# Q and K transposed by DMA instead of TensorE and VectorE in a fused attention and feed-forward kernel

## Chip, cores, metric

One core of one Trainium2 chip. The metric is the device time of one execution in microseconds (us), the median of several runs. Brackets behind a time give the lowest and the highest run, those behind a ratio a 95% interval.

## The reference, cut to what matters

Block-sparse attention (4 batches, 8 heads, 768 tokens, head size 64), then a gated feed-forward layer with RMS norm over 512 channels.

```python
scores = scale * q @ k.T                    # per batch and head, masked by blocks of 32 tokens
attn   = softmax(scores);  x = attn @ v     # x: [3072 tokens, 512]
xn     = x / rms(x) * rms_g
out    = (silu(xn @ w_gate) * (xn @ w_val)) @ w_out      # d_ff = 1536
```

## The kernel before

The work goes by *units*: half of the queries of one batch, all eight heads, as four *pairs* of heads. There are 8 units of 12 *steps*. A step issues two score tiles, their exp (ScalarE) and their mask (VectorE); attention times V follows. The feed-forward work of an earlier unit is cut into small items and dealt out between steps to fill TensorE. All of it is one fixed program order per engine.

TensorE needs Q and K with the head dimension on the partitions. The loads bring tokens on the partitions, so every pair is transposed: 24 TensorE transposes into PSUM, then one copy by VectorE.

```python
def load_qk(b, lo, hi):                              # issued on POOL; float32 -> bfloat16
    nc.gpsimd.dma_start(out=qraw[b][:, lo:hi, :], in_=qv[b, :, lo:hi, :])
    nc.gpsimd.dma_start(out=kraw[b][:, lo:hi, :], in_=kv[b, :, lo:hi, :])

def transposes(b, pr, early=False):
    ...
    t_ = ps_s.tile([P, 2, 1024], BF16, name="tqk", tag="s")   # one of the two PSUM slots of the scores
    tt = [t_[:, 0, :], t_[:, 1, :]]
    for i, src in enumerate((qraw[b], kraw[b])):
        for c in range(NC):                          # NC = 6 chunks of 64 columns
            for h in range(2):
                nc.tensor.transpose(out=tt[i][64*h:64*h+64, c*P:(c+1)*P],
                                    in_=src[:, 2*pr+h, c*D:(c+1)*D], identity=ident)
    nc.vector.tensor_copy(out=x, in_=t_[:, :, 0:S])
```

POOL has two roles. It issues all loads, and it makes two small things that TensorE needs at the end of a unit: the squares of the attention output for the RMS norm, and the norm's power of -1/2.

```python
# in av(), once per pair:
    nc.scalar.copy(out=osb[u][:, pr, :], in_=o_)
    nc.gpsimd.tensor_tensor(out=o2s[u][:, pr, :], in0=osb[u][:, pr, :],
                            in1=osb[u][:, pr, :], op=ALU.mult)            # the square
# norm_a(u): TensorE sums the four squares;  norm_b(u), on POOL:
    nc.gpsimd.tensor_tensor(out=rs, in0=ms, in1=nhalf, op=ALU.pow)        # the power, "rs"
```

The plan: `at(step, cost, fn, ...)` puts a piece of work at a step. The cost is the planner's guess of TensorE time. It sets how many feed-forward items are dealt out there.

```python
for b in range(1, B):
    for pr, sl in enumerate((7, 8, 9, 10) if b == 1 else (2, 4, 6, 7)):
        at(3 * (8 * (b - 1) + sl) + 2, 0.95, transposes, b, pr)
    at(3 * 8 * (b - 1) + 1, 0, load_qk, b, 0, H)
    at(3 * (8 * (b - 1) + (1 if b == 1 else 4)) + 1, 0, load_v, b)
at(4, 0, load_wo)
...
    for cost, fn, a in todo:
        fn(*a)
        credit -= cost
        if fn in (transposes, norm_d, norm_e):
            tail = 1.2                               # deal out this much feed-forward work behind it
```

The softmax here doesn't subtract the row's maximum and nothing guards it: scores larger than these inputs give would overflow.

## Time and profile before

| | before |
|---|---|
| median of 3 runs | 387.07 us (386.75 to 387.38) |
| span of the profiled run | 387.4 us |
| TensorE / VectorE / ScalarE / POOL busy | 90% / 67% / 57% / 15% |
| TensorE time of one transpose block | 0.80 us, 12 blocks for batches 1 to 3 |
| VectorE copy of one block | 0.95 us |

From the page of before: busy times, the slices (40 equal parts of the span, busy share in tenths), and the packets of the software queue (POOL's loads) and the hardware queue (SP's transfers).

```profile
span 387.4 us, 6807 instructions
PE 348.7 (90%) x2742; PEld 165.6 (43%) x2742; DVE 259.0 (67%) x539; ACT 222.5 (57%) x353; POOL 59.5 (15%) x88
...
PE   3678788998699899999999999999999999999995
...
DMA  5999960065001500075002400000000000000012
...
q0 software_dynamic: 16208, 14.16, 23.7%
q1 hardware_dynamic: 4020, 6.30, 4.3%
```

TensorE is at 90% or more from slice 15 (136 us) up to the last slice. DMA is full in slices 2 to 5 and partly in 6: weights, V and the first two batches.

From the page's groups (line, engine, operation, out<-in, count, busy us, mean ns, idle before): the transposes and their copy. The count of 13 is the 12 blocks and the first pair of batch 0.

```profile
L168 DVE COPY qkT<-tqk 128x1536 bf16<-128x1536 bf16 x13 | 12.3, 951 | 0.9 <-PE tqk L161 0.9
L161 PE MATMUL tqk<-ident,qb 128*64 128x128 bf16 x156 | 7.2, 229 | 5.5 <-DMA qb<-in_q_dram 4.8
```

From the timeline of before, one block in the steady state (start, length, engine, line):

```profile
192.81 0.53 PE L161 MATMUL tqk<-ident,qb 128*64 128x128 bf16 x12
...
193.61 0.82 PE L405 MATMUL yp<-wo,hp 128*128 128x512 bf16 x3
...
194.33 0.95 DVE L168 COPY qkT<-tqk 128x1536 bf16<-128x1536 bf16 x1
```

The block starts at 192.81 and the next TensorE work at 193.61: 0.80 us.

From the list of waits of TensorE between 60 us and the end (us, times, longest): score matmuls that waited for a copy, since the transposes held a score slot.

```profile
PE s__1097 L235 <- DVE qkT L168: 1.0, 1, 1.0
...
PE s__941 L235 <- DVE qkT L168: 0.8, 1, 0.8
...
PE s__1252 L235 <- DVE qkT L168: 0.7, 1, 0.7
...
PE s__2797 L235 <- DVE qkT L168: 0.4, 1, 0.4
PE s__1952 L235 <- DVE qkT L168: 0.4, 1, 0.4
```

These sum to 3.3 us.

### The profile page before, as it was taken

Reading aid. Unit: us, or ns where it says so; the run is one execution under the profiler, and the core shown is the slowest. Engines: PE = TensorE matmul, PEld = TensorE weight load, DVE = VectorE, ACT = ScalarE, POOL = GpSimd, SP = SyncE. Lnnn points to the kernel's source line nnn. Section 1 sums busy time; section 2 is a strip of 40 time slices with the busy share of each in tenths; the row PEclk is TensorE's granted clock in tenths of the full one; section 3 lists DMA queues with packets and bytes.
Section 4 is the critical chain, followed back from the end, with each engine's and each line's share of the span. In section 5 each row is a group of like instructions: output and inputs, shape, how many; then the busy total and the mean of one; then the engine's idle time right before and its main releaser. Section 6 shows DMA issues by size and latency. Waiting matters only on the chain.

```text
span 387.4 us, 6807 instructions
## 1 busy us (share of the span) xinstructions
PE 348.7 (90%) x2742; PEld 165.6 (43%) x2742; DVE 259.0 (67%) x539; ACT 222.5 (57%) x353; POOL 59.5 (15%) x88
## 2 busy tenths in 40 slices
PE   3678788998699899999999999999999999999995
PEld 1223233444344444454444544444444444455552
DVE  4866675778675877677766777767666776566540
ACT  2357765666556466567666665667667767232331
POOL 8921010131011100021101100010010110100000
PEclk9998867999999999999999999999999999999999
DMA  5999960065001500075002400000000000000012
GB/s 72 178 209 207 205 111 1 0 83 83 0 2 34 77 29 27 2 120 99 3 27 40 71 27 29 2 28 30 0 29 27 29 0 29 28 29 28 29 50 86
DMA packets 20259, 20.88 MB, mean 54 GB/s; under 512 B 1284, under 2 KB 17156, under 8 KB 20228
## 3 DMA queue, kind: packets, MB, share of 16 engines
q0 software_dynamic: 16208, 14.16, 23.7%
q1 hardware_dynamic: 4020, 6.30, 4.3%
q8 instruction: 21, 0.34, 0.4%
q14 instruction: 10, 0.08, 0.1%
HBM read 28.31 MB, written 6.29 MB: 89 GB/s over the span
## 4 chain that ended last, share of the span: by engine, by line
PE 66%; DVE 18%; ACT 11%; issue 3%; DMA 1%; POOL 0%; DVEq 0%; ACTq 0%; POOLq 0%
PE yp L405 13%; PE gp L374 11%; PE vp L391 11%; ACT pt L242 8%; DVE pt L248 6%; PE zw L283 5%; PE oa L267 3%; DVE uu L380 3%; ACT th L378 3%; DVE hp L394 2%; DVE xn L359 2%; PE tqk L161 1%; DVE qkT L168 1%; DMA kb<-in_k_dram 1%; PE vw L391 1%
## 5 line engine op out<-in xcount | busy, mean ns | idle before, releaser
L248 DVE TENSOR_TENSOR pt<-pt,Mk 128x768 bf16<-128x768 bf16 x192 | 101.1, 554 | 23.9 <-ACT pt L242 19.3
L380 DVE SCALAR_TENSOR_TENSOR uu<-th,gp 128x384 bf16<-128x384 bf16 x90 | 49.7, 553 | 57.4 <-ACT th L378 57.1
L378 ACT ACTIVATE th<-gp 128x384 bf16<-128x384 f32 x90 | 44.2, 492 | 62.0 <-PE gp L374 59.9
L405 PE MATMUL yp<-wo,hp 128*128 128x512 bf16 x288 | 76.2, 380 | 0.0
L391 PE MATMUL vp<-xn,wv 128*128 128x384 bf16 x360 | 74.2, 329 | 2.1 <-DVE hp L394 1.8
L374 PE MATMUL gp<-xn,wg 128*128 128x384 bf16 x360 | 74.5, 330 | 1.4 <-DVE xn L359 0.8
L394 DVE TENSOR_TENSOR hp<-uu,vp 128x384 bf16<-128x384 bf16 x90 | 49.8, 553 | 19.6 <-PE vp L391 14.2
L374 PEld LDWEIGHTS <-wg 128*128 128x128 bf16 x384 | 35.4, 99 | 36.5 <-issue 11.0
L391 PEld LDWEIGHTS <-wv 128*128 128x128 bf16 x384 | 35.0, 98 | 31.9 <-issue 12.3
L235 PEld LDWEIGHTS <-qkT 64*128 64x128 bf16 x384 | 14.6, 95 | 55.8 <-issue 47.5
L405 PEld LDWEIGHTS <-hp 128*128 128x128 bf16 x288 | 25.5, 98 | 28.2 <-issue 7.3
L267 PEld LDWEIGHTS <-vb 128*64 128x64 bf16 x384 | 22.6, 116 | 18.6 <-issue 12.1
L411 ACT ACTIVATE yo<-yp 128x512 f32<-128x512 f32 x24 | 14.3, 598 | 20.1 <-PE yp L405 19.8
L283 PE MATMUL zw<-pt,Ez 128*32 128x384 bf16 x384 | 23.3, 352 | 0.0
L359 DVE SCALAR_TENSOR_TENSOR xn<-osb,gcol,fb 128x384 bf16<-128x384 f32 x28 | 15.9, 608 | 0.0
L318 POOL TENSOR_TENSOR rs<-ms,nhalf 128x3 f32<-128x3 f32 x8 | 7.1, 889 | 48.0 <-DVE ms L315 48.0
L267 PE MATMUL oa<-pt,vb 128*64 128x384 bf16 x96 | 13.7, 441 | 0.0
L283 PEld LDWEIGHTS <-Ez 128*32 128x32 bf16 x384 | 7.6, 99 | 13.5 <-issue 11.9
L168 DVE COPY qkT<-tqk 128x1536 bf16<-128x1536 bf16 x13 | 12.3, 951 | 0.9 <-PE tqk L161 0.9
L161 PE MATMUL tqk<-ident,qb 128*64 128x128 bf16 x156 | 7.2, 229 | 5.5 <-DMA qb<-in_q_dram 4.8
L161 PEld LDWEIGHTS <-qb 128*64 128x64 bf16 x192 | 6.6, 116 | 9.7 <-issue 4.8
L183 PE MATMUL mp<-Qvis,Kind 24*128 24x384 bf16 x12 | 5.3, 482 | 3.6 <-DVE Qvis L179 2.5
(556 smaller groups left out, 433.0 us busy)
## 6 DMA issues: line engine op xcount, KB each, us to landing
out_dram<-yo SPq DMA_DIRECT2D x24, 256.0 KB, 2.0
vb<-in_v_dram POOLq DMA_DIRECT2D x4, 768.0 KB, 7.9
qb<-in_q_dram POOLq DMA_DIRECT2D x3, 768.0 KB, 8.0
kb<-in_k_dram POOLq DMA_DIRECT2D x3, 768.0 KB, 10.7
wg<-in_moe_w_gate_dram POOLq DMA_DIRECT2D x2, 768.0 KB, 13.0
wv<-in_moe_w_val_dram POOLq DMA_DIRECT2D x2, 768.0 KB, 16.6
wo<-in_moe_w_out_dram POOLq DMA_DIRECT2D x1, 1536.0 KB, 28.5
qb<-in_q_dram POOLq DMA_DIRECT2D x2, 192.0 KB, 3.5
```

The source lines that it names most:

```text
L161: nc.tensor.transpose(out=tt[i][64 * h:64 * h + 64, c * P:(c + 1) * P], in_=src[:, 2 * pr + h, c * D:(c + 1) * D], identity=ident)
L242: nc.scalar.activation(out=ptiles[n][:, jt, :, :], in_=s_[:, :, 0:TG], func=AF.Exp, scale=SCALE)
L248: nc.vector.tensor_tensor(out=pv, in0=pv, in1=Mk[:, jt, ic * TG:(ic + 1) * TG].unsqueeze(1).to_broadcast([P, 2, TG]), op=ALU.mult)
L267: nc.tensor.matmul(out=o_[64 * e:64 * e + 64, :], lhsT=vb[:, 2 * pr + e, jt * D:(jt + 1) * D], rhs=pt_[:, jt, e, :], start=(jt == 0), stop ...
L283: nc.tensor.matmul(out=zwt[u][32 * c:32 * c + 32, :], lhsT=Ez[:, pr, :], rhs=pt_[:, 2 * j2 + par, e, :], start=(pr == 0 and j2 == 0), stop ...
L359: nc.vector.scalar_tensor_tensor(out=xns[u][:, pr, :], in0=osb[u][:, pr, :], scalar=gcol[:, pr:pr + 1], in1=fb[i], op0=ALU.mult, op1=ALU.mult)
L374: nc.tensor.matmul(out=gp, lhsT=wg[:, c, f * P:(f + 1) * P], rhs=xns[u][:, c, :], start=(c == 0), stop=(c == NP - 1))
L378: nc.scalar.activation(out=th, in_=gp, func=AF.Tanh, scale=0.5)
L380: nc.vector.scalar_tensor_tensor(out=uu, in0=th, scalar=1.0, in1=gp, op0=ALU.add, op1=ALU.mult)
L391: nc.tensor.matmul(out=vp, lhsT=wv[:, c, f * P:(f + 1) * P], rhs=xns[u][:, c, :], start=(c == 0), stop=(c == NP - 1))
L394: nc.vector.tensor_tensor(out=hps[u][:, f, :], in0=uu, in1=vp, op=ALU.mult)
L405: nc.tensor.matmul(out=yp, lhsT=hps[u][:, f, t * P:(t + 1) * P], rhs=wo[:, f, :], start=(f == 0), stop=(f == NF - 1))
```

## The change

The intent: take 12 transpose blocks off the busiest engine and 12 copies off VectorE, using a DMA transpose on the SP queue, which is nearly idle. A DMA transpose wants a pair's two heads interleaved by chunk, so the loads write them so: four DMAs per pair (Q and K, two heads each) with rows of 128 B in SBUF, where before two DMAs per batch wrote rows of 768 B.

```diff
-    qkpool = ctx.enter_context(tc.tile_pool(name="qkpool", bufs=6))
+    qkpool = ctx.enter_context(tc.tile_pool(name="qkpool", bufs=8))
...
+    def load_pair(b, pr):
...
+        for t, src in ((qraw[b], qv), (kraw[b], kv)):
+            dst = t[:, 2 * pr:2 * pr + 2, :].rearrange("p h w -> p (h w)").rearrange(
+                "p (c h d) -> p h c d", c=NC, h=2)
+            sp = src[b, :, 2 * pr:2 * pr + 2, :].rearrange("p h (c d) -> p h c d", c=NC)
+            for h in range(2):
+                nc.gpsimd.dma_start(out=dst[:, h], in_=sp[:, h])
...
+    def transposes_dma(b, pr):
+        x = qkpool.tile([P, 2, S], BF16, name="qkT", tag="qkT")
+        qk[(b, pr)] = x
+        for i, src in enumerate((qraw[b], kraw[b])):
+            nc.sync.dma_start_transpose(
+                out=x[:, i, :].rearrange("q (c p) -> q c p", c=NC),
+                in_=src[:, 2 * pr:2 * pr + 2, :].rearrange("p h w -> p (h w)"))
...
     for b in range(1, B):
-        for pr, sl in enumerate((7, 8, 9, 10) if b == 1 else (2, 4, 6, 7)):
-            at(3 * (8 * (b - 1) + sl) + 2, 0.95, transposes, b, pr)
-        at(3 * 8 * (b - 1) + 1, 0, load_qk, b, 0, H)
+        for pr in range(NP):
+            at(3 * (8 * (b - 1) + pr) + 1, 0, load_pair, b, pr)
+            at(3 * (8 * (b - 1) + pr + (3 if b == 1 else 2)) + 1, 0, transposes_dma, b, pr)
```

## The prediction

> **What bounds the kernel now.** TensorE. The page gives it 348.7 of 387.4 us (90%); VectorE 67%, ScalarE 57%, POOL 15%. In the table by stretches TensorE is busy 19.2 to 19.8 us of every 20 from 160 us on, but only 16.8 to 18.6 between 80 and 160 us. The chain of waits is 66% TensorE. DMA is full (about 205 GB/s written) from 8 to 54 us and mostly idle later.
>
> **What goes away.** Twelve blocks of 24 TensorE transposes. The timeline around single blocks shows 0.80 us from a block's first matmul to the next work: 12 x 0.80 = 9.6 us of TensorE. Twelve VectorE copies of 951 ns = 11.4 us. The list of waits from 60 us on has five waits of TensorE for such a copy (score matmuls that needed the PSUM slot which the transposes held), 3.3 us in all, and transposes that waited 0.7 us for the exp. All this is on the in-order TensorE stream: 13 to 14 us. VectorE's 11.4 us is mostly off the chain.
>
> **What is added.**
> (a) Loads: a pair's Q and K become 4 DMAs of 768 packets of 128 B written (256 B read) in place of packets of 768 B: 12,288 per batch for 2,048. Software-queue packets cost 23.7% x 16 x 387 / 16,208 = 90 ns each on average. If a small one costs 45 to 90 ns (estimate), a pair takes 9 to 17 us of all 16 engines, a batch 35 to 70 us, where its period is about 87 us. POOL issues cost 0.72 to 0.98 us whatever the size: 48 for 6, +36 us of a 15% busy engine.
> (b) 24 DMA transposes of 128x768. The Trainium skill, "VectorE: DVE Perf Modes", section "The three transpose paths", gives 1309 ns for 128x128 by DMA; no run here shows it yet. Six blocks are then at most 8 us, 24 transposes up to 190 us of the SP queue, which now issues only 24 stores. They are issued 14 or more steps (about 3.5 us each) before their first use.
>
> **Critical path.** Steady state hides both. The tight place is batch 1: its loads share the full DMA queue with weights, V and the output weight. I estimate that its last pair lands at 85 to 110 us; its first use is at step 33, about 112 us in before, less the gain. So perhaps 0 to 5 us of new waiting there, or more at the bad end. Stores behind transposes on SP can be late by a few us; three output buffers cover that.
>
> **Prediction.** 13.5 us off, some 2 us given back by new waits on ScalarE and VectorE and by batch 1: 376 us. Range 368 to 386. Faster by over 2%: 65%; within 2%: 22%; slower: 13%.
>
> **What would show it right.** TensorE busy about 339 us, the 951 ns copies down from 13 to 1, no score matmul waiting for them; gain spread over 73 to 248 us; VectorE near 247 us; packets near 47,000; DMA transposes under 8 us each; no score matmul waiting on a transpose DMA. Up to 60 us the two traces should be alike.
>
> **What would make it wrong.** Small packets or transposes that take several times my estimates, so that score matmuls of batch 1 wait for a transposed tile; POOL blocked when too many descriptors are outstanding, so that the squares or the norm's power come late and TensorE waits at the norm; SP held so long that stores, then ScalarE's output copies, stall; or TensorE's removed time turning into waits for exp and mask, so that the gain shrinks below 2%.

## More of the kernel before

Last, POOL's timeline of before where the start's loads and the squares of unit 0 (`o_322`) meet:

```profile
17.50 0.92 POOL L70 DMA_DIRECT2D qb<-in_q_dram  x1
...
25.32 0.83 POOL L273 TENSOR_TENSOR o_322<-osb 128x384 bf16<-128x384 f32 x1 [6.03 <-ACT osb L272]
26.10 0.94 POOL L75 DMA_DIRECT2D vb<-in_v_dram  x1
27.03 1.02 POOL L133 DMA_DIRECT2D wo<-in_moe_w_out_dram  x1
...
37.34 0.82 POOL L273 TENSOR_TENSOR o_322<-osb 128x384 bf16<-128x384 f32 x1 [5.39 <-ACT osb L272]
43.96 0.83 POOL L273 TENSOR_TENSOR o_322<-osb 128x384 bf16<-128x384 f32 x1 [5.80 <-ACT osb L272]
49.97 1.06 POOL L318 TENSOR_TENSOR rs<-ms,nhalf 128x3 f32<-128x3 f32 x1 [5.18 <-DVE ms L315]
```

POOL never waits for a DMA here. Each square waits only for ScalarE's copy, and the power of unit 0 comes at 49.97 us.

## The result and the profile after

392.38 us median (392.12 to 393.07, 3 runs) against 387.07. The ratio to before is 1.0141, interval 1.0117 to 1.0165. A ratio is the mean time of one kernel's runs over that of the other's of the same rounds, so not quite the ratio of the medians quoted. The change made the kernel 1.4% slower: clear of the noise, though less than the 2% at which a run counts as slower here.

The page after:

```profile
span 390.7 us, 6305 instructions
PE 332.0 (85%) x2426; PEld 157.2 (40%) x2454; DVE 249.2 (64%) x527; ACT 222.1 (57%) x353; POOL 93.4 (24%) x130
...
PE   2687508798879999998989898999899899999995
...
DMA  5999999008866930053999520000000000000012
...
q0 software_dynamic: 47600, 14.16, 35.0%
q1 hardware_dynamic: 23220, 11.02, 12.2%
```

The removed work is gone: VectorE 259 to 249 us, TensorE 348.7 to 332.0. (This trace lacks 28 records of the output matmuls. The page's idle time before these is 3.5 us, so TensorE's time is nearer 335.5; plain16 below, with the same matmul list and all records, has 335.9.) But slices 5 and 6 of TensorE's row, 39 to 59 us, have fallen to 5 and 0, from 7 and 8 before: a hole. The list of waits of TensorE names it:

```profile
PE zw L312 <- POOL o_324 L293: 13.9, 1, 13.9
PE vp L411 <- DVE hp L414: 5.4, 11, 0.9
...
PE gp L394 <- DVE uu L400: 4.3, 9, 1.2
```

TensorE waits 13.9 us once, for a POOL square. POOL's timeline after, the same place as above:

```profile
25.41 0.82 POOL L293 TENSOR_TENSOR o_324<-osb 128x384 bf16<-128x384 f32 x1 [4.48 <-ACT osb L292]
26.19 0.88 POOL L83 DMA_DIRECT2D qb<-in_q_dram  x1
28.98 0.82 POOL L83 DMA_DIRECT2D qb<-in_q_dram  x1 [1.92 <-DMA wv<-in_moe_w_val_dram]
32.24 0.82 POOL L83 DMA_DIRECT2D kb<-in_k_dram  x1 [2.44 <-DMA wg<-in_moe_w_gate_dram]
35.96 0.82 POOL L83 DMA_DIRECT2D kb<-in_k_dram  x1 [2.90 <-DMA wv<-in_moe_w_val_dram]
...
37.72 1.03 POOL L145 DMA_DIRECT2D wo<-in_moe_w_out_dram  x1
38.74 0.90 POOL L293 TENSOR_TENSOR o_324<-osb 128x384 bf16<-128x384 f32 x1
...
42.94 0.84 POOL L293 TENSOR_TENSOR o_324<-osb 128x384 bf16<-128x384 f32 x1
...
47.33 0.82 POOL L83 DMA_DIRECT2D kb<-in_k_dram  x1 [1.92 <-DMA vb<-in_v_dram]
57.01 0.82 POOL L83 DMA_DIRECT2D kb<-in_k_dram  x1 [8.86 <-DMA wo<-in_moe_w_out_dram]
57.84 0.84 POOL L293 TENSOR_TENSOR o_324<-osb 128x384 bf16<-128x384 f32 x1
63.26 1.05 POOL L338 TENSOR_TENSOR rs<-ms,nhalf 128x3 f32<-128x3 f32 x1 [4.57 <-DVE ms L335]
```

The bracket is POOL's idle time and what ended it. At the issue of a small load POOL waits until an *earlier, unrelated* DMA has landed: the weights, V, and last for 8.86 us the output weight `wo`. The last square of unit 0 stands behind that in POOL's order and runs at 57.84 us; the power follows at 63.26 us, 13.3 us later than before.

Counting POOL's load issues in program order shows the rule: each waits for the completion of the DMA issued eight before it. The instruction list agrees: POOL's DMA issues take eight completion semaphores (DMASW0 to DMASW7) in turn, and from the ninth on each waits on its own. The semaphore numbers in the traces of before and after show the same. So the 17th to 19th DMA (pair 1) wait for the 9th to 11th (three weight pieces), the 28th for the 20th (V), the 29th (last of pair 3) for the 21st (`wo`). The Trainium skill, "DMA: Bandwidth & Descriptors", section "Why a DMA increments its semaphore by 16 and not by 1", asks for "One semaphore per in-flight slot, not one per stream"; here the program has eight such slots.

The second reading is a table of unit lengths: the distance from one `rs` on POOL's timeline to the next (us). "First" is the first `rs`, "tail" the rest of the span.

| kernel | first | 0-1 | 1-2 | 2-3 | 3-4 | 4-5 | 5-6 | 6-7 | sum of units | tail |
|---|---|---|---|---|---|---|---|---|---|---|
| before | 50.0 | 36.84 | 44.52 | 43.37 | 41.89 | 43.89 | 40.70 | 36.13 | 287.3 | 50.1 |
| after | 63.3 | 31.93 | 42.28 | 41.40 | 42.36 | 42.34 | 42.35 | 35.84 | 278.5 | 48.9 |

The late start costs 13.3 us. The units give back 8.8 and the tail 1.2, so the span is 3.3 us longer (390.7 against 387.4). The medians differ by more, 5.3 us: the profiled execution of before took 389.08 us, more than any of its three timed runs. (The plan deals the feed-forward work out over units, so early columns are best read in sum.) Column 5-6 is strange: that unit had no transposes in either kernel, and no loads or DMA transposes run in it, yet it takes 42.35 in place of 40.70 us. Something costs 1.65 us a unit that is neither DMA nor transposes.

Unit 0-1 needs a caution: the TensorE clock that was granted there differs between runs (0.88 of full speed in before, 0.98 in after; from unit 2-3 to 6-7 it was 1.00 in both). before and loads_only (below) have the same matmul list, and their unit 0-1 takes 36.84 us at 0.88 and 34.31 us at 0.99. So some 2.5 us of a difference between two sums can be clock.

### The profile page after: what moved, and what is told of

It reads as the page before. It is cut to its first block, busy times and chain, and to the rows that moved or that the text cites. A ratio compares the mean times of both kernels' runs of the same rounds, so it can differ in the third digit from the quotient of the medians.

```text
span 390.7 us, 6305 instructions
## 1 busy us (share of the span) xinstructions
PE 332.0 (85%) x2426; PEld 157.2 (40%) x2454; DVE 249.2 (64%) x527; ACT 222.1 (57%) x353; POOL 93.4 (24%) x130
## 2 busy tenths in 40 slices
DMA packets 70850, 25.58 MB, mean 65 GB/s; under 512 B 58020, under 2 KB 67748, under 8 KB 70820
## 3 DMA queue, kind: packets, MB, share of 16 engines
q0 software_dynamic: 47600, 14.16, 35.0%
q1 hardware_dynamic: 23220, 11.02, 12.2%
## 4 chain that ended last, share of the span: by engine, by line
PE 50%; DVE 19%; ACT 11%; DMA 10%; issue 4%; POOL 4%; POOLq 0%; DVEq 0%; ACTq 0%
PE gp L394 10%; PE yp L425 10%; PE vp L411 9%; ACT pt L262 7%; DVE pt L268 7%; DMA wo<-in_moe_w_out_dram 5%; DMA wv<-in_moe_w_val_dram 5%; DVE uu L400 5%; PE zw L303 4%; ACT th L398 3%; DVE xn L379 3%; DVE hp L414 3%; PE oa L287 1%; PE vw L411 1%; PE gw L394 1%
## 5 line engine op out<-in xcount | busy, mean ns | idle before, releaser
L425 PE MATMUL yp<-wo,hp 128*128 128x512 bf16 x260 | 70.8, 381 | 3.5 <-issue 3.1
L411 PEld LDWEIGHTS <-wv 128*128 128x128 bf16 x384 | 36.0, 99 | 35.3 <-issue 14.5
L287 PEld LDWEIGHTS <-vb 128*64 128x64 bf16 x384 | 21.4, 114 | 18.0 <-issue 11.0
L83 POOL DMA_DIRECT2D kb<-in_k_dram x24 | 19.6, 819 | 16.3 <-DMA wo<-in_moe_w_out_dram 8.9
L431 ACT ACTIVATE yo<-yp 128x512 f32<-128x512 f32 x24 | 14.3, 597 | 15.3 <-PE yp L425 13.6
L83 POOL DMA_DIRECT2D qb<-in_q_dram x24 | 20.5, 856 | 1.9 <-DMA wv<-in_moe_w_val_dram 1.9
L312 PE MATMUL zw<-o_324,Ew 128*32 128x384 bf16 x4 | 0.8, 372 | 13.9 <-POOL o_324 L293 13.9
L316 DVE COPY zs<-zw 128x384 f32<-128x384 f32 x8 | 4.4, 551 | 12.7 <-PE zw L312 12.7
L287 PE MATMUL oa<-pt,vb 128*64 128x384 bf16 x96 | 12.2, 404 | 0.0
```

The source lines that it names most:

```text
L83: nc.gpsimd.dma_start(out=dst[:, h], in_=sp[:, h])
L287: nc.tensor.matmul(out=o_[64 * e:64 * e + 64, :], lhsT=vb[:, 2 * pr + e, jt * D:(jt + 1) * D], rhs=pt_[:, jt, e, :], start=(jt == 0), stop ...
L411: nc.tensor.matmul(out=vp, lhsT=wv[:, c, f * P:(f + 1) * P], rhs=xns[u][:, c, :], start=(c == 0), stop=(c == NP - 1))
L425: nc.tensor.matmul(out=yp, lhsT=hps[u][:, f, t * P:(t + 1) * P], rhs=wo[:, f, :], start=(f == 0), stop=(f == NF - 1))
```

## The experiments

I held two theories. **A**: the 13 us at the start come from POOL's order, a load that waits for the DMA eight before it, with a square behind it. **B**: the missing gain in the units comes from the new order of the feed-forward items, because the planner lost the blocks' costs. Rivals: the DMA transposes or the small packets themselves slow the engines or the queue.

### late3: one pair's load moved

```diff
-            at(3 * (8 * (b - 1) + pr) + 1, 0, load_pair, b, pr)
+            at(15 if (b, pr) == (1, 3) else 3 * (8 * (b - 1) + pr) + 1, 0, load_pair, b, pr)
-            at(3 * (8 * (b - 1) + pr + (3 if b == 1 else 2)) + 1, 0, transposes_dma, b, pr)
+            at(24 if (b, pr) == (1, 3) else
+               3 * (8 * (b - 1) + pr + (3 if b == 1 else 2)) + 1, 0, transposes_dma, b, pr)
```

> Edit: the changed kernel with only the load of batch 1's fourth pair moved from step 10 to step 15, and its transposes from step 19 to 24 (first use at step 33). Every packet and every transpose stays. Theory A (POOL waited at a load's issue for the DMA issued eight before it, the output weight, and the square that TensorE needed stood behind it): TensorE's wait for that square falls from 13.9 us to under 2 us, the time to 379 to 384 us. Rival (the full DMA queue itself, or transposes beside loads, delays the start, whatever the order on POOL): the first 64 us stay as long and the time stays above 389 us.

Measured: 378.02 us (377.65 to 381.46), ratio to before 0.9788 (0.9732 to 0.9843). POOL's timeline of late3:

```profile
43.56 0.82 POOL L293 TENSOR_TENSOR o<-osb 128x384 bf16<-128x384 f32 x1 [0.48 <-ACT osb L292]
49.56 1.06 POOL L338 TENSOR_TENSOR rs<-ms,nhalf 128x3 f32<-128x3 f32 x1 [5.18 <-DVE ms L335]
...
51.38 1.75 POOL L83 DMA_DIRECT2D qb<-in_q_dram  x2
...
56.46 0.82 POOL L83 DMA_DIRECT2D kb<-in_k_dram  x1 [2.52 <-DMA wo<-in_moe_w_out_dram]
```

The wait for `wo` is still there (2.52 us) but behind it stands no square that TensorE needs at that moment. The power is back at 49.56 us, and the wait of TensorE for a square is not in its list any more. `wo` landed at 56.2 us, as late as in after (56.7), so the queue ahead of it was no emptier. Every packet and every transpose stayed, so 14.4 us of the 392.38 were the order on POOL. The time is 1 us better than the range that I had written. Theory A holds.

### plain16 and plain2: packet size and number of DMAs

plain16 keeps 16 DMAs per batch but writes rows of 768 B; plain2 takes the two load DMAs of before. Both keep the DMA transposes, and both transpose the wrong blocks on purpose (two chunks of one head).

```diff
 # plain16, in load_pair
-            dst = t[:, 2 * pr:2 * pr + 2, :].rearrange(...)   # interleaved
-            sp = src[b, :, 2 * pr:2 * pr + 2, :].rearrange(...)
+            dst = t[:, 2 * pr:2 * pr + 2, :]
+            sp = src[b, :, 2 * pr:2 * pr + 2, :]
 # plain2, in the plan
-            at(3 * (8 * (b - 1) + pr) + 1, 0, load_pair, b, pr)
+        at(3 * 8 * (b - 1) + 1, 0, load_qk, b, 0, H)
```

> Edit: the changed kernel with its 16 load DMAs per batch at their places, but heads not interleaved: packets of 768 B written in place of 128 B. Result wrong on purpose, as in plain2. If small packets lengthen the queue ahead of the output weight, it lands near 47 us in place of 57 us and TensorE's wait for the square is 2 to 5 us, the time 381 to 385 us. If the number of DMAs alone makes the wait, it stays at 10 us or more and the time above 389 us. If packets are all of it, the wait is gone and the time is 378 to 380 us.

> Edit: the changed kernel with the loads of before (2 DMAs per batch, 768 B packets, heads not interleaved) and the DMA transposes kept. Result wrong on purpose: the transposed blocks hold two chunks of one head in place of one chunk of two heads; sizes and types are equal. Theory A and B: no wait for the square, the new order's loss remains, 378 to 382 us. Rival (the DMA transposes themselves cost): 387 us or more.

Measured: plain16 391.20 us (390.06 to 392.29), ratio 1.0098 (1.0064 to 1.0133); plain2 378.58 us (377.59 to 380.03), ratio 0.9776 (0.9739 to 0.9812). plain16 went against my first expectation: `wo` landed at 56.5 us (issued at 36.6, 19.9 us to landing), as in after (56.7). The wait of TensorE in plain16:

```profile
PE zw L311 <- POOL o L292: 13.1, 1, 13.1
```

and of POOL up to 75 us:

```profile
POOL kb L82 <- DMA wo<-in_moe_w_out_dram: 9.0, 1, 9.0
POOL kb L82 <- DMA vb<-in_v_dram: 4.6, 1, 4.6
```

So the size of the packets does not make the wait; the number of DMAs, and where they stand between the squares, does, through the eight semaphores. (plain2 changes both the number and the places; late3 has the 16 DMAs and changes a place alone.) plain2 has only 2 DMAs for batch 1, POOL shows no wait for a DMA up to 75 us, and the time is 14 us under after. plain2 and late3 agree within 0.6 us although one has 128 B packets and the other has not, and their units from 1-2 on agree within 0.02 us each: once POOL's order is right, the small packets cost nothing that can be seen.

Both wrong kernels passed the comparison with the reference. Q and K are drawn with a factor of 0.1, so I take it that the softmax is nearly even and hides them; no run tests this. It means that the comparison says little about a transpose.

### loads_only: the new loads with TensorE's transposes

```diff
-            at(3 * (8 * (b - 1) + pr + (3 if b == 1 else 2)) + 1, 0, transposes_dma, b, pr)
+            at(3 * (8 * (b - 1) + ((7, 8, 9, 10) if b == 1 else (2, 4, 6, 7))[pr]) + 2, 0.95, transposes, b, pr)
 # and transposes() reads the interleaved layout for b > 0
```

> Edit: the changed kernel's loads alone (interleaved, 16 DMAs per batch, 128 B packets), the transposes by TensorE and VectorE at their old places and costs, TensorE's order as in before. Theory A: the wait for the square of about 13 us stays and nothing is gained: 398 to 402 us. Rival (the transposes on the SP queue take part in the wait): the wait is under 8 us, below 396 us.

Measured: 397.63 us (395.65 to 399.95), ratio 1.0299 (1.0256 to 1.0341). The median is just under my range. In the profiled run, which is its fastest, TensorE's wait for the square is 8.3 us, not 13; all units from 1-2 on are those of before within 0.01 us. The loads alone make the kernel slower than the whole change does. The rival has a part: without DMA transposes `wo` lands 15.5 us after its issue in place of 19.0 (at 52.6 in place of 56.7 us). The transposes of pairs 0 and 1 run just then, on the same 16 DMA engines as the full load queue.

### wo_late: the other end of the wait

```diff
-    at(4, 0, load_wo)
+    at(15, 0, load_wo)
```

> Edit: the changed kernel with only the load of the output weight moved from step 4 to step 15, so that no load of batch 1 has it eight DMAs ahead; the four pairs stay where they are. Theory A: POOL's waits of 8.9 us for the output weight and 1.9 us for V are gone, TensorE's wait for the square is under 2 us, 377 to 381 us as late3. Rival (the fourth pair's DMAs as such, not what they wait for, delay the square): the wait stays above 8 us and the time above 386 us.

Measured: 382.27 us (381.31 to 384.17), ratio 0.9888 (0.9857 to 0.9919). The pairs stayed where they were; only the DMA eight before changed. POOL's wait for `wo` is gone, TensorE's wait falls to 2.8 us and the first `rs` comes at 52.5 us. The direction is A's, but the time is 1.3 us above my range and the wait 0.8 us above; POOL still waits for V (1.2 us) and for the weight pieces there, and the issues take time themselves: between the second square (37.04 us) and the fourth (47.09 us) POOL spends 6.7 us on eight of them. This edit also takes `wo` out of the full queue, so by itself it does not separate the semaphores from the queue; late3, where `wo` stays, does.

### hold: the old order of TensorE

```diff
+    def hold():
+        pass
...
+        for sl in (7, 8, 9, 10) if b == 1 else (2, 4, 6, 7):
+            at(3 * (8 * (b - 1) + sl) + 2, 0.95, hold)
...
-            if fn in (transposes, norm_d, norm_e):
+            if fn in (transposes, hold, norm_d, norm_e):
```

> Edit: the changed kernel with an empty step of cost 0.95 left in the interleaving plan at each place where the twelve TensorE transpose blocks stood, so that the feed-forward work is dealt out as before: TensorE's instructions are then exactly those of before, in that order, less the transposes. The 13.9 us wait near 45 us stays. Theory B (the missing gain in the steady state is the new order of the feed-forward work): units that took 42.3 us take 40 to 41 us, the time is 382 to 386 us, waits of vp for hp and gp for uu fall from 9.7 us to under 4 us. Rival (transposes and small packets slow the engines): units stay at 42.3 us, also those after 240 us only if the rival is wrong; the time stays at 391 to 393 us.

Measured: 387.14 us (386.67 to 388.09), ratio to before 0.9997 (0.9967 to 1.0027), 5.2 us under after. That is 1 us above my range; the start's hole (13.1 us) stayed as expected. TensorE's instruction list equals that of before without the transposes, line by line. The waits of hold:

```profile
PE zw L315 <- POOL o L296: 13.1, 1, 13.1
...
PE vp L414 <- DVE hp L417: 3.1, 9, 1.1
...
PE gp L397 <- DVE uu L403: 0.9, 3, 0.5
```

Waits of `vp` for `hp` and of `gp` for `uu` fell from 9.7 to 4.0 us, the edge of what I had expected: with one PSUM slot for each, two gate items too close together make TensorE wait for ScalarE and VectorE. The units:

| kernel | first | 0-1 | 1-2 | 2-3 | 3-4 | 4-5 | 5-6 | 6-7 | sum of units |
|---|---|---|---|---|---|---|---|---|---|
| hold | 63.3 | 36.03 | 39.37 | 39.11 | 40.99 | 40.68 | 40.70 | 36.12 | 273.0 |
| before_cheap | 49.5 | 33.58 | 45.67 | 44.25 | 43.23 | 44.94 | 42.36 | 35.84 | 289.9 |
| late3_hold | 48.8 | 34.30 | 39.38 | 39.10 | 40.99 | 40.68 | 40.71 | 36.12 | 271.3 |

Unit 5-6 is back at 40.70 us. Unit 3-4, in which most of batch 3's loads and DMA transposes run, takes 40.99, only 0.3 us more than 5-6, in which none run. Against before, hold's units are 14.3 us shorter in sum, and 13.5 us from 1-2 on, where the granted clock was 1.00 in both: the gain that was predicted, present in full and spent again at the start. Theory B holds; contention in the steady state does not.

### before_cheap: the new order without the new transposes

```diff
 # in the kernel before
-            at(3 * (8 * (b - 1) + sl) + 2, 0.95, transposes, b, pr)
+            at(3 * (8 * (b - 1) + sl) + 2, 0, transposes, b, pr)
...
-            if fn in (transposes, norm_d, norm_e):
+            if fn in (norm_d, norm_e):
```

> Edit: the kernel before, TensorE transposes kept, but their cost in the interleaving plan set to 0 and the extra feed-forward work behind each left out, so that TensorE's order is exactly that of the changed kernel plus the transposes. Loads and DMA as before. Theory B (the order alone costs about 5 us): 390 to 394 us, the unit without transposes before the last takes 42.3 us in place of 40.7. Rival (the order is harmless and DMA traffic makes the 42.3 us units): 386 to 388 us and 40.7 us.

Measured: 388.92 us (388.23 to 389.97), ratio 1.0056 (1.0029 to 1.0082). Unit 5-6 takes 42.36 us, within 0.01 of after, in a kernel with no DMA transpose at all: the order is the cause of that figure. The total is 1 us under my range; the order costs 2.5 us in the sum of units here (289.9 against 287.3), and 5.5 us without the transposes (after 278.5 against hold 273.0). Part of this difference is clock: unit 0-1 was granted 0.94 in before_cheap and 0.88 in before. Against loads_only, which has the matmul list of before and was granted 0.99 there, before_cheap's sum is 5.1 us longer (289.9 against 284.8). Whether the cost of the order depends on the transposes stays open.

### late3_hold: both repairs

The two edits of late3 and hold together.

> Edit: both repairs together: batch 1's fourth pair loaded at step 15 and transposed at step 24, and the empty steps of cost 0.95 where the transpose blocks stood. From hold's units (36.03, 39.37, 39.11, 40.99, 40.68, 40.70, 36.12 us) and late3's first unit (49.6 us), if the two causes add: 372 to 375 us, 3.3% faster than before. If they overlap (the order costs only behind the wait, or the wait hides the order): 376 to 379 us.

Measured: 373.16 us (371.81 to 375.2, 6 runs) against 386.98, ratio 0.9648 (0.9619 to 0.9677). It beats both kernels. The two savings add: 392.38 less 14.4 (late3) less 5.2 (hold) is 372.8.

```profile
span 370.1 us, 6304 instructions
...
PE   3697687989799989999999999999999999999995
```

From the page of late3_hold: slices 5 and 6, the hole, are back at 6 and 8, with the same 70,850 packets as after, and TensorE is full from slice 16 (139 us) on, where the row of after alternates between 8 and 9.

## Why the prediction was wrong

- **The gain from removing the work, 13.5 us, was right.** With TensorE's old order kept (hold), the units are 14.3 us shorter, 13.5 of it from unit 1-2 on; with both repairs (late3_hold) the whole kernel is 13.8 us faster than before.
- **The step that failed is "Critical path. Steady state hides both. The tight place is batch 1 ... perhaps 0 to 5 us of new waiting there".** It looked for the wait in the wrong queue: score matmuls waiting for late data. No score matmul waited for a tile transposed by DMA. The wait was at POOL's issue: 48 loads were costed as 48 issues of at most 0.98 us, and the term for waiting at an issue was left at zero. It measured 18.0 us of POOL waiting (8.9 + 4.8 + 2.4 + 1.9), and TensorE waited 13.9 us for the square behind the last of these. I had named "POOL blocked when too many descriptors are outstanding, so that the squares ... come late" as a way to be wrong, without giving it time. It was close, but plain16, with few packets and as long a wait, shows that DMAs count and not descriptors. The program of before already gives POOL's loads eight semaphores in turn; I read that only afterwards.
- **The second failed term is "some 2 us given back by new waits on ScalarE and VectorE".** I did not ask what the planner does when a cost of 0.95 becomes 0. The new order costs 5.2 us (after against hold).
- **The added DMA costs were too high.** Packets: after has 30,720 more software-queue packets than plain16 and its queue took 35.0% of 390.7 us against 25.0% of 389.5, that is 39.4 us of 16 engines or 630 us of one. With the 6,144 plain packets that they replace at 90 ns, 36,864 small ones took (630 + 553) / 36,864 = 32 ns each (an estimate; the packet records of after's trace give a mean of 32.4 ns), not 45 to 90. Transposes: the hardware queue rose from 4.3% to 12.2%, 31 us over 24, so 1.3 us of all engines each on average, not up to 8. (Three pairs of transposes that ran with the loads idle, in windows of 2.60 us from 95.3, 140.5 and 211.4 us, show a DMA share of 0.79 to 0.80: about 1.03 us each.) The Trainium skill, "VectorE: DVE Perf Modes", section "The three transpose paths", from which I took 1309 ns per 128x128 and multiplied by six, was not a figure to scale by.
- **"Packets near 47,000" held for the loads** (47,600); I forgot the transposes' own 19,200. "Up to 60 us the two traces should be alike" was false: POOL's issues differ from 17.5 us on, and TensorE's hole begins at 44.8 us.
- POOL's rise (59.5 to 93.4 us busy) and VectorE's fall were as forecast.

## What to carry to other kernels

Before a load is split into more DMAs, find out how many completions its queue can have open, and what else stands behind its issue on that engine: a load that waits there stops the compute instructions behind it, even if its own data is not wanted for 50 us. When work is taken out of a kernel whose order was tuned by costs, keep the old order first and tune it afterwards, so that what is measured is the removal. A change can hold its full gain and lose it elsewhere; unit by unit lengths show it where the total does not.

## What the Trainium skill lacked or had wrong

- "DMA: Bandwidth & Descriptors" has the idea of a semaphore per in-flight slot, but not what it costs when a program's slots run out and the next issue stops its engine. Here POOL waited up to 8.9 us at one issue and 18.0 us in all.
- No page gives a measured time for one 128 B packet in a long load on POOL's queue. Here such packets took about 32 ns each (above), and the kernels with them (late3, 378.02 us) and without (plain2, 378.58 us) were alike.
- "VectorE: DVE Perf Modes", section "The three transpose paths", gives one figure per 128x128 tile. For 128x768 the trace of after shows a median of 1.23 us of SP issue (1.21 to 5.3 us, the longest while the load queue was full), a median of 2.8 us (K) and 3.6 us (Q) to landing, and 1.3 us of all 16 engines on average, about 1.03 us with the loads idle.
- "Advanced Engine Details and Errata", section "X-Bar Transpose (TRN2)", expects 350 to 400 GB/s. These small transposes did not reach that: 196,608 B in 1.03 us, with the loads idle, is about 190 GB/s, and in the mean 1.3 us about 150 GB/s (estimates from the DMA shares). The full load queue of before wrote about 205 GB/s. No run here has a larger transpose.
- "DMA: Bandwidth & Descriptors", section "Rules for kernel authors", says, in a row on corrupted data, that a transpose next to ordinary DMAs needs nothing; it does not say that the transpose takes time from them. Here `wo` landed 4.1 us later with the transposes (56.7) than without (52.6, loads_only), in one profiled execution each.
